# mLSTM and feed-forward on one core: a new order for the first group, a sigmoid moved, the second weights after the gates

## The chip, the cores and the metric

The kernel runs on one core of a Trainium2 chip. A core has five engines that run side by side, each on its own queue of instructions: TensorE (PE: matrix products, with PEld for its weight loads), VectorE (DVE), ScalarE (ACT), GpSimd (POOL) and SyncE (SP), which here only issues DMAs. The metric is the device time of one execution in microseconds. Before the change the median of three runs is 504.06 us (502.53 to 504.66).

## The reference, cut to what matters

Four batches with eight heads, 768 tokens and head dimension 40 go through an mLSTM recurrence; its output, 3072 tokens of 320 channels, goes through a feed-forward layer of width 2048. All is float32.

```python
def _attn_ref(q, k, v, i_gate, f_gate, o_gate):
    for t in range(S):
        m_new = np.maximum(f_gate[:, :, t] + m, i_gate[:, :, t])
        f_stab = np.exp(f_gate[:, :, t] + m - m_new)
        i_stab = np.exp(i_gate[:, :, t] - m_new)
        C = f_stab * C + i_stab * outer(v_t, k_t)
        n = f_stab * n + i_stab * k_t
        h_tilde = C @ q_t
        denom = np.maximum(np.abs(n . q_t), 1.0)
        o = 1.0 / (1.0 + np.exp(-o_gate[:, :, t]))
        y[:, :, t] = o * h_tilde / denom

def _moe_ref(x, w_in, w_out, alpha):
    h = x @ w_in
    g = np.maximum(h, 0.0) + alpha * np.minimum(h, 0.0)
    return g @ w_out
```

(The products with axes are abbreviated.)

## The kernel before, in words

**Attention.** Each batch is cut into 6 chunks of 128 tokens (n = 0 to 23 over all batches, c is the chunk within its batch, b the batch). Within a chunk the recurrence becomes a masked product: scores pS = K q, times a decay matrix E, times v; from the chunks before comes a state C. For each chunk stage_a makes q and k by channel (transposes on PE, copies on ACT), and stage_b makes, in two parities of four heads, the decay (exponentials L418 on ACT, a mask L422 on POOL), the scores on PE and their weighing, then the values pH (PE). gated_steps (L377) divides by the denominator, multiplies by the sigmoid of the output gate, og, (L392, on DVE, on POOL from chunk 6 on) and writes x as xn (L394), whose last 64 channels it copies once more behind themselves (L398, on POOL). From chunk 6 on the operands are split into three bfloat16 parts: score_parts (L322) and values_by_parts (L331), with casts on ACT (L327) in between.

**The output gate's sigmoid** is taken for a whole batch of six chunks at once by open_gate (L124): in stage_b, at the batch's first chunk, after the second parity's mask. Its data is loaded by load_gate when the batch before has ended, as there is one buffer. Exp and Sigmoid use different function tables of ACT; L126 is preceded by a table load, and so is the next Exp. Batch 0 takes it in two pieces in the opening order (og1, og2).

**Feed-forward.** Two chunks form a group g of 256 tokens (GC = 2, 12 groups). stage_x transposes x and splits it into high and low parts (XH, XL, X2, X2L). FeedForward.up (L576) makes in each of 8 steps fp two blocks of 128 hidden channels, eight products each (L585 to L592), then Relu on ACT (L594), the negative slope on DVE (L598), a high part gh on ACT (L606) and a low part gl (L607, on DVE for g < 2, on POOL after that). FeedForward.down (L610) adds into po (L615).

**Weights.** w_in comes in blocks of 512 columns (two row tiles wi and the remaining rows wr), w_out in pairs of 128 rows (wo). Each is fetched as raw words, and Weights.scale (L688, ACT), join in two steps (L700 and L702, DVE), high (L710, ACT) and low (L714, DVE) convert it. w[0], w[1], w[2] are block 0 of w_in (w[2] holds the remaining rows of blocks 0 and 1), w[3] and w[4] are block 1. The raw words lie in rooms shared with other weights, so the load of block 2's remaining rows waits until w[3]'s raw words have been read.

**The opening.** first_group (L803) builds the gates (cumulative sums L, decays) and the first group. Its steps have names, and the string ORDER (L559) says in which order they are issued. pin (L778) chains all of these instructions on each engine in that order, SP's DMAs included; queue (L790) puts everything issued until feed-forward step 2 behind the last of them. Beyond that the scheduler of the framework chooses the order on each engine. A step warmN (L939) issues N bfloat16 products of the identity into a PSUM tile that nobody reads. The steps that the text speaks of: dq, dv, dw, do, dx, dL are loads; lf, li, L, bj, wt are rows of the gates; qT/qc and kT/kc transpose and copy q and k; sp spreads a row of L over the partitions (PE, L890), ex takes its exponentials (ACT, L901), ms masks them (POOL, L905), sc are scores, wg weighs them (DVE, L925); bT, wT, eT turn gates to columns; wd is k weighed (kd, L139), u0 the state's update; v0 and v1 the values; g0r to g1p the steps of gated_steps; x0, x1 the transposes of x; s0, s1 their split (L481 to L485); w0 to w2 the conversions of weights; lpa to lpe split the sums of chunks 2 and 3. row and pick are copies of parts of the identity (L840, L841) that the spreads of chunks 1 to 3 use as weights.

After ORDER, first_group makes the rest of the gates for chunks 2 to 5 (L1099 to L1114); before the change the conversions of block 1 of w_in stand ahead of that (L1093 to L1095).

Of the kernel before, what the change touches and what calls it, by code (L numbers as in the profile page):

```python
# [8 lines left out]
F32 = mybir.dt.float32  # L9
# [8 lines left out]
def kernel(ctx: ExitStack, tc: tile.TileContext, q, k, v, i_gate, f_gate, o_gate, w_in, w_out, alpha, out):  # L18
# [105 lines left out]
    def open_gate(b, c0=0, c1=NC):  # L124
        og = o_tiles[b][:, c0:c1]
        nc.scalar.activation(og, og, AF.Sigmoid)  # L126
# [168 lines left out]
    def values(n, E, busy=lambda: None):  # L295

        pH = psa(f"pH{n}")
        va = va_t[n // GC % NV][:, n % GC]
        for i in range(H):
            if i % 2 == 0:  # L300
                busy()
            par, p = divmod(i, NPR)
            h = 2 * p + par
            nc.tensor.matmul(
                pH[:, h * VA : (h + 1) * VA], E[par][:, p * P : (p + 1) * P], va[:, h], start=True, stop=True
            )
        return pH[:, : H * VA].rearrange("p (h e) -> p h e", e=VA)
# [64 lines left out]
    def gated(n, hv):  # L372

        for _ in gated_steps(n, hv):
            pass

    def gated_steps(n, hv):  # L377
# [19 lines left out]
        yield  # L397
        nc.gpsimd.tensor_copy(xn[:, j, DM:], xn[:, j, 2 * P : DM])  # L398
        yield

    def stage_b(n):
# [4 lines left out]
        for par in range(2):  # L406
# [18 lines left out]
            )  # L425
            if c == 0 and par == 1:
                open_gate(b)
            pS = psa(f"pS{n}_{par}")
# [18 lines left out]
        if c > 0:  # L447
            *_, T = from_state(n, qf, Q)
        hv = values(n, Es) if n < NBF else values_by_parts(n, Es)
        if c > 0:  # L450
            nc.vector.tensor_tensor(T, T, hv, ALU.add)
            hv = T
        gated(n, hv)
        if c == NC - 1 and n + 1 < B * NC:
            load_gate(b + 1, nc.sync)
# [57 lines left out]
    def attention(n0):  # L513
# [44 lines left out]
    V0, V1 = 0, 2  # L558
    ORDER = """dq0 dq1 dw0 dw2 warm24 dv0 dw1 dw4 do1 dw3 do2 scan lf0a lf0b li0 lf0z L0 bj0 qT0 qc0 kT0 kc0 warm12 sp00  # L559
        bTt bTc l3a l3b alT l3c l3d warm6 wt0 ex00 sc00 l3e ms00 warm3 sp01 ewj ex01 ms01 sc01 warm3 eeL wg00 wTt eTt  # L560
        wTc eTc lf1a lf1b warm3 w0s wg01 sp10 alC ex10 ms10 warm3 sp11 ex11 qT1 w1s kT1 kc1 w0j0 warm4 li1 wd0 w0j1 w2s
        u0m qc1 u0c v0 w0h w0l w1j0 L1 w2j0 warm2 sc10 w1j1 warm2 w2j1 wd1 wg10 fsm fst sc11 ms11 warm6 dv1 dq3 wg11 og1
        lpa lpb bj1 dq2 dL dx2 w1h g0r dx0 g0g lpc lpd lpe g0x g0p w1l dx1 v1 x0 warm4 tadd g1r g1g s0a w2h g1x g1p w2l x1
        s1a s1d warm3 s0d og2"""

# [237 lines left out]
    def first_group():  # L803
# [34 lines left out]
        row = const.tile([3 * BH, BH], F32R, tag="row", name="row")  # L838
        for j in range(3):
            nc.vector.tensor_copy(row[j * BH : (j + 1) * BH], ident[j * BH : (j + 1) * BH, j * BH : (j + 1) * BH])  # L840
        nc.vector.tensor_copy(pick, row.bitcast(F32))  # L841

# [170 lines left out]
        def later_decays():  # L1013
# [16 lines left out]
        steps.update(  # L1030
            scan=scan_m,

            lf0z=lambda: nc.vector.memset(lf[0][:, 0:1], 0.0),
            lf0a=lambda: first_lf(0, t0, nc.vector), lf0b=lambda: second_lf(0, u0, nc.vector),
            lf1a=lambda: first_lf(1, t1, nc.gpsimd), lf1b=lambda: second_lf(1, u1, nc.gpsimd),
            li0=lambda: nc.gpsimd.tensor_tensor(li[:, t0], i[:, t0], m[:, u0], ALU.subtract),
            li1=lambda: nc.gpsimd.tensor_tensor(li[:, t1], i[:, t1], m[:, u1], ALU.subtract),
# [54 lines left out]
        weights(GC, NC, nc.gpsimd)  # L1092
        for t in w[3:]:  # L1093
            t.all()
        w[2].split(1)  # L1095
        yield


# [13 lines left out]
        nc.tensor.matmul(pg[:R, : BH * NC], ones, gd.rearrange("p a c -> p (a c)"), start=True, stop=True)  # L1112
        nc.vector.tensor_copy(gamB[:R].rearrange("p a c -> p (a c)"), pg[:R, : BH * NC])
        update(1)  # L1114
        yield
# [88 lines left out]
```

## Time and profile before

| | |
|---|---|
| median of three runs | 504.06 us |
| lowest and highest | 502.53 and 504.66 us |
| the profiled execution's own time | 500.96 us |
| its span, first to last instruction | 499.2 us |
| mean granted clock of TensorE in it | 0.99 |
| instructions | 11801 |

The profile is of one execution. The span is what the engines' rows add up in; 1.76 us of the execution lie around it. PE's granted clock is a share of 2.4 GHz: 1.00 is 2.4 GHz, 0.50 is 1.2 GHz. A row's idle time in brackets is what its engine waited just before it, with the name of what ended the wait, as far as semaphores tell it.

### The profile page before, as it was taken

Reading aid. Unit: us, or ns where it says so; the run is one execution under the profiler, and the core shown is the slowest. Engines: PE = TensorE matmul, PEld = TensorE weight load, DVE = VectorE, ACT = ScalarE, POOL = GpSimd, SP = SyncE. Lnnn points to the kernel's source line nnn. Section 1 sums busy time; section 2 is a strip of 40 time slices with the busy share of each in tenths; the row PEclk is TensorE's granted clock in tenths of the full one; section 3 lists DMA queues with packets and bytes.
Section 4 is the critical chain, followed back from the end, with each engine's and each line's share of the span. In section 5 each row is a group of like instructions: output and inputs, shape, how many; then the busy total and the mean of one; then the engine's idle time right before and its main releaser. Section 6 shows DMA issues by size and latency. Waiting matters only on the chain.

```text
span 499.2 us, 11801 instructions
## 1 busy us (share of the span) xinstructions
PE 477.7 (96%) x4463; PEld 457.2 (92%) x4463; DVE 321.6 (64%) x676; ACT 321.6 (64%) x700; POOL 304.8 (61%) x393
## 2 busy tenths in 40 slices
PE   8889889989999999999899999999999999999997
PEld 7778879989989999989799999989999999999997
DVE  6889999934577686764395686567586575642321
ACT  3869697656587677756976677677886673343332
POOL 6632262306469889839498789858878755243242
PEclk9989997999999999999999999999999999999999
DMA  9999976345676566597557575769663130000000
GB/s 169 228 189 278 229 203 183 82 79 125 145 181 146 92 166 156 102 166 158 116 143 135 129 141 121 162 166 156 117 175 83 32 97 1 1 27 1 28 1 26
DMA packets 173922, 61.60 MB, mean 123 GB/s; under 512 B 140154, under 2 KB 166122, under 8 KB 173866
## 3 DMA queue, kind: packets, MB, share of 16 engines
q1 hardware_dynamic: 173786, 60.75, 55.3%
q8 instruction: 35, 0.57, 0.5%
q14 instruction: 21, 0.17, 0.1%
q10 hardware_dynamic: 80, 0.11, 0.1%
HBM read 36.90 MB, written 4.03 MB: 82 GB/s over the span
## 4 chain that ended last, share of the span: by engine, by line
PE 62%; DVE 8%; DMA 8%; ACT 8%; SPq 6%; issue 3%; POOL 3%; ACTq 0%; DVEq 0%; POOLq 0%
PE po L615 25%; PE ph L585 4%; PE ph L588 3%; PE ph L586 3%; PE ph L589 3%; PE ph L591 3%; PE ph L587 3%; PE ph L592 3%; PE ph L590 3%; DMA wo<-in_moe_w_out_dram 3%; PE pH L340 3%; PE pS L434 2%; SPq L678 2%; ACT E L418 2%; SPq L122 2%
## 5 line engine op out<-in xcount | busy, mean ns | idle before, releaser
L607 POOL TENSOR_TENSOR gl<-g,gh 128x512 fp32r<-128x512 f32 x80 | 102.9, 1287 | 62.2 <-ACT gh L606 55.0
L598 DVE SCALAR_TENSOR_TENSOR g<-g,oma,ph 128x256 f32<-128x256 f32 x160 | 69.8, 476 | 76.9 <-ACT g L594 73.1
L615 PE MATMUL po<-OH,gh 128*128 128x320 f32 x368 | 111.3, 314 | 0.0
L615 PE MATMUL po<-OL,gh 128*128 128x320 f32 x368 | 109.6, 311 | 0.0
L594 ACT ACTIVATE g<-ph 128x512 f32<-128x512 f32 x96 | 57.2, 596 | 43.7 <-PE ph L592 31.8
L615 PE MATMUL po<-OH,gl 128*128 128x320 f32 x368 | 71.9, 316 | 1.3 <-POOL gl L607 1.3
L606 ACT CAST gh<-g 128x512 fp32r<-128x512 f32 x80 | 49.5, 619 | 33.3 <-DVE g L598 32.0
L615 PEld LDWEIGHTS po<-OH,gh 128*128 128x128 f32 x368 | 69.0, 188 | 0.4 <-ACT gh L606 0.2
L615 PEld LDWEIGHTS po<-OL,gh 128*128 128x128 f32 x368 | 69.2, 188 | 0.2 <-DVE OL L714 0.2
L585 PE MATMUL ph<-XH,WH 128*128 128x256 f32 x192 | 58.5, 305 | 1.3 <-DVE g L598 0.9
L615 PEld LDWEIGHTS po<-OH,gl 128*128 128x128 f32 x368 | 56.9, 188 | 1.8 <-POOL gl L607 1.8
L418 ACT ACTIVATE E<-Lb,bT 128x128 f32<-128x128 f32 x160 | 50.9, 393 | 7.5 <-PE pH L340 7.2
L589 PE MATMUL ph<-X,W 128*128 128x256 f32 x192 | 55.2, 288 | 0.0
L586 PE MATMUL ph<-XH,WH 128*128 128x256 f32 x192 | 54.9, 286 | 0.0
L588 PE MATMUL ph<-XH,WL 128*128 128x256 f32 x192 | 54.6, 284 | 0.0
L591 PE MATMUL ph<-XL,WH 128*128 128x256 f32 x192 | 54.6, 284 | 0.0
L592 PE MATMUL ph<-X2L,W 128*128 128x256 f32 x192 | 54.5, 285 | 0.0
L587 PE MATMUL ph<-XH,WL 128*128 128x256 f32 x192 | 54.4, 284 | 0.0
L590 PE MATMUL ph<-XL,WH 128*128 128x256 f32 x192 | 54.2, 282 | 0.0
L422 POOL TENSOR_SCALAR_AFFINE_SELECT E<-E 128x512 f32<-128x512 f32 x44 | 30.0, 683 | 36.4 <-ACT E L418 36.4
L327 ACT CAST E<-pS 128x512 bf16<-128x512 f32 x72 | 41.8, 585 | 13.9 <-DVE pS L325 9.1
L585 PEld LDWEIGHTS ph<-XH,WH 128*128 128x128 f32 x192 | 36.6, 191 | 2.3 <-issue 1.1
(198 smaller groups left out, 1146.0 us busy)
## 6 DMA issues: line engine op xcount, KB each, us to landing
Lb<-L_d SPq DMA_DIRECT2D x20, 512.0 KB
wo<-in_moe_w_out_dram SPq DMA_DIRECT2D x8, 640.0 KB
wi<-in_moe_w_in_dram SPq DMA_DIRECT2D x8, 512.0 KB
qn<-in_q_dram SPq DMA_DIRECT2D x24, 160.0 KB
kn<-in_k_dram SPq DMA_DIRECT2D x24, 160.0 KB
va<-in_v_dram SPq DMA_DIRECT2D x24, 160.0 KB
og<-in_o_gate_dram SPq DMA_DIRECT2D x24, 160.0 KB
out_dram<-ob SPq DMA_DIRECT2D x11, 320.0 KB
```

The costliest lines, as they stand in the source:

```text
L418: nc.scalar.activation(E[:, p * P : (p + 1) * P], Lb[:, h] if Lb is not None else pb[:, p * P : (p + 1) * P], AF.Exp, bias=bT[:, c, b * H ...
L585: nc.tensor.matmul(dst, WH[half][:, 0, hs], XH[:, 0], start=True, stop=False)
L586: nc.tensor.matmul(dst, WH[half][:, 1, hs], XH[:, 1], start=False, stop=False)
L587: nc.tensor.matmul(dst, WL[half][:, 0, hs], XH[:, 0], start=False, stop=False)
L588: nc.tensor.matmul(dst, WL[half][:, 1, hs], XH[:, 1], start=False, stop=False)
L589: nc.tensor.matmul(dst, W2[:, fs], X2, start=False, stop=False)
L590: nc.tensor.matmul(dst, WH[half][:, 0, hs], XL[:, 0], start=False, stop=False)
L591: nc.tensor.matmul(dst, WH[half][:, 1, hs], XL[:, 1], start=False, stop=False)
L592: nc.tensor.matmul(dst, W2[:, fs], X2L, start=False, stop=True)
L598: nc.vector.scalar_tensor_tensor(out=y[:, e], in0=gt[:, e], scalar=oma[:, f : f + 1], in1=ph[:, e], op0=ALU.mult, op1=ALU.add)
L607: (nc.vector if g < 2 else nc.gpsimd).tensor_tensor(gl, y, gh.bitcast(F32), ALU.subtract)
L615: nc.tensor.matmul(po[j], x[:, e, j * P : (j + 1) * P], W[f // NB][:, f % NB], **ends)
```

## The change: what it does

Six edits:

- gated_steps: the copy of x's last channels is done by DVE instead of POOL in group 0.
- stage_b: open_gate for a batch's first chunk moves from the second parity to behind the values, and is taken in two pieces: chunks 0 and 1 ahead of the gating, chunks 2 to 5 behind it.
- ORDER is another one. 24 warming products at its head become 12; both q are transposed ahead of the first spread; the later q, k, scores and masks of chunk 1 come before the values of chunk 0; ten warming products stand between the transposes of x's two halves.
- row and pick are copied by ACT, as a step rowc of ORDER, instead of by DVE ahead of it.
- li0 moves from POOL to DVE.
- The conversions of block 1 of w_in move behind the rest of the gates.

```diff
@@ gated_steps @@
-        nc.gpsimd.tensor_copy(xn[:, j, DM:], xn[:, j, 2 * P : DM])
+        (nc.vector if g == 0 else nc.gpsimd).tensor_copy(xn[:, j, DM:], xn[:, j, 2 * P : DM])
@@ stage_b @@
-            if c == 0 and par == 1:
-                open_gate(b)
             pS = psa(f"pS{n}_{par}")
...
         hv = values(n, Es) if n < NBF else values_by_parts(n, Es)
+
+        if c == 0:
+            open_gate(b, 0, GC)
         if c > 0:
             nc.vector.tensor_tensor(T, T, hv, ALU.add)
             hv = T
         gated(n, hv)
+        if c == 0:
+            open_gate(b, GC, NC)
@@ ORDER @@
-    ORDER = """dq0 dq1 dw0 dw2 warm24 dv0 dw1 dw4 do1 dw3 do2 scan lf0a lf0b li0 lf0z L0 bj0 qT0 qc0 kT0 kc0 warm12 sp00
-        bTt bTc l3a l3b alT l3c l3d warm6 wt0 ex00 sc00 l3e ms00 warm3 sp01 ewj ex01 ms01 sc01 warm3 eeL wg00 wTt eTt
-        wTc eTc lf1a lf1b warm3 w0s wg01 sp10 alC ex10 ms10 warm3 sp11 ex11 qT1 w1s kT1 kc1 w0j0 warm4 li1 wd0 w0j1 w2s
-        u0m qc1 u0c v0 w0h w0l w1j0 L1 w2j0 warm2 sc10 w1j1 warm2 w2j1 wd1 wg10 fsm fst sc11 ms11 warm6 dv1 dq3 wg11 og1
-        lpa lpb bj1 dq2 dL dx2 w1h g0r dx0 g0g lpc lpd lpe g0x g0p w1l dx1 v1 x0 warm4 tadd g1r g1g s0a w2h g1x g1p w2l x1
-        s1a s1d warm3 s0d og2"""
+    ORDER = """dq0 dq1 dw0 dw2 rowc warm12 dv0 dw1 dw4 do1 dw3 do2 scan lf0a lf0b lf0z L0 li0 bj0 qT0 qc0 kT0 kc0 warm3
+        qT1 qc1 warm10 l3a l3b sp00 bTt bTc sp01 wt0 ewj ex00 l3c l3d wTt l3e wTc ms00 sc00 ex01 wd0 wg00 ms01 kT1 lf1a w0s
+        sc01 warm2 u0m wg01 lf1b eeL sp10 u0c kc1 eTt w0j0 ex10 sp11 eTc w0j1 ms10 warm2 sc10 ex11 ms11 sc11 warm2 v0 wg10
+        L1 w1s fsm og1 wg11 alT w1j0 alC g0r li1 wd1 fst w0h w1j1 bj1 dv1 dq3 v1 lpa g0g g0x g0p lpb w2s w0l warm4 x0 tadd
+        g1r g1g g1x g1p s0a warm10 lpc lpd lpe w2j0 dq2 dL dx0 dx1 dx2 w1h x1 w2j1 s1a w2h s0d w1l s1d w2l warm6 og2"""
@@ first_group @@
-        for j in range(3):
-            nc.vector.tensor_copy(row[j * BH : (j + 1) * BH], ident[j * BH : (j + 1) * BH, j * BH : (j + 1) * BH])
-        nc.vector.tensor_copy(pick, row.bitcast(F32))
+
+        def picks():
+            for j in range(3):
+                nc.scalar.copy(row[j * BH : (j + 1) * BH], ident[j * BH : (j + 1) * BH, j * BH : (j + 1) * BH])
+            nc.scalar.copy(pick, row.bitcast(F32))
...
-            li0=lambda: nc.gpsimd.tensor_tensor(li[:, t0], i[:, t0], m[:, u0], ALU.subtract),
+            li0=lambda: nc.vector.tensor_tensor(li[:, t0], i[:, t0], m[:, u0], ALU.subtract),
...
         weights(GC, NC, nc.gpsimd)
-        for t in w[3:]:
-            t.all()
-        w[2].split(1)
-        yield
...
         nc.vector.tensor_copy(gamB[:R].rearrange("p a c -> p (a c)"), pg[:R, : BH * NC])
+        for t in w[3:]:
+            t.all()
+        w[2].split(1)
+        yield
         update(1)
```

## Rows read from the trace of the kernel before

**Rows 1.** The page's first part: busy us, share of the span, instructions, by engine.
```profile
PE 477.7 (96%) x4463; PEld 457.2 (92%) x4463; DVE 321.6 (64%) x676; ACT 321.6 (64%) x700; POOL 304.8 (61%) x393
```

**Rows 2.** Windows: length, busy us of PE, PEld, DVE, ACT, POOL; clock, DMA share, GB/s.
```profile
12.00:33.00 21.00, 17.33 (x157) 14.99 (x157) 18.32 (x36) 14.06 (x32) 12.37 (x14) 0.99 1.13 224
33.00:45.00 12.00, 11.18 (x104) 10.01 (x103) 9.89 (x25) 10.93 (x22) 1.40 (x2) 0.87 0.77 225
45.00:70.00 25.00, 23.17 (x213) 21.36 (x211) 23.54 (x47) 20.27 (x49) 9.04 (x11) 1.00 0.92 229
```

**Rows 3.** Windows again: two at the lower clock, three around later sigmoids.
```profile
32.60:36.00 3.40, 3.40 (x18) 3.40 (x17) 2.59 (x8) 3.36 (x5) 0.00 (x0) 0.50 0.33 120
...
73.60:80.40 6.80, 6.80 (x34) 6.80 (x34) 6.71 (x13) 6.67 (x16) 3.04 (x4) 0.50 0.99 294
...
106.00:111.00 5.00, 3.39 (x26) 3.13 (x25) 1.09 (x2) 4.06 (x4) 0.00 (x0) 1.00 0.00 2
...
236.00:243.00 7.00, 4.70 (x45) 4.40 (x44) 1.88 (x4) 5.10 (x8) 3.12 (x5) 1.00 0.69 128
...
346.00:354.00 8.00, 8.00 (x89) 7.75 (x86) 4.01 (x11) 7.86 (x17) 5.56 (x8) 1.00 1.14 200
```

**Rows 4.** PE's waits: line waited for, us in total, times, longest.
```profile
PE pH L340 <- ACT E L327: 3.6, 3, 2.3
...
PE po L615 <- ACT gg L606: 1.6, 1, 1.6
```

**Rows 5.** Timeline of ACT at sigmoids: start, us, instruction [idle before, releaser].
```profile
106.30 1.28 ACT L126 ACT_TABLE_LOAD   x1 [1.53 <-DMA og<-in_o_gate_dram]
107.59 1.80 ACT L126 ACTIVATE og<-og 128x1920 f32<-128x1920 f32 x1
...
237.94 1.28 ACT L126 ACT_TABLE_LOAD   x1 [1.89 <-DMA C<-C]
...
349.49 1.28 ACT L126 ACT_TABLE_LOAD   x1
```

**Rows 6.** Timeline of PE up to the first spread.
```profile
1.43 4.67 PE L942 MATMUL warm<-ident 128*128 128x256 bf16 x24 [1.43 <-POOL ident masks.py:199]
...
6.89 1.47 PE L942 MATMUL warm<-ident 128*128 128x256 bf16 x12
...
8.29 1.15 PE L890 MATMUL pb<-g_L,ident 32*128 32x128 f32 x8
```

**Rows 7.** Timeline of ACT: its first copy and first exponentials.
```profile
6.57 0.58 ACT L874 COPY qf<-pqk 104x512 f32<-104x512 f32 x1 [3.56 <-PE pqk L218]
...
9.83 1.14 ACT L901 ACTIVATE E<-pb,bT 128x128 f32<-128x128 f32 x4 [1.56 <-DVE bT L860]
```

**Rows 8.** Timeline of DVE from wT to the last split of x.
```profile
14.34 0.22 DVE L860 COPY wT<-ps_gw 128x64 f32<-128x64 f32 x1 [1.61 <-PE ps_gw L856]
...
15.96 3.02 DVE L139 TENSOR_TENSOR kd<-kn,wT 128x320 f32<-128x320 f32 x1
...
21.87 1.21 DVE L978 TENSOR_TENSOR_SCAN g_L<-g_WL,g_lf 32x512 f32<-32x512 f32 x1
...
29.99 0.49 DVE L394 TENSOR_TENSOR xn<-T,og 128x320 f32<-128x320 f32 x1
...
32.55 0.28 DVE L485 TENSOR_TENSOR X2L<-p,X 128x128 fp32r<-128x128 f32 x1
```

**Rows 9.** Timeline of POOL beside DVE's kd.
```profile
17.55 1.08 POOL L1037 TENSOR_TENSOR g_li<-g_WH,g_WL 32x512 f32<-32x512 f32 x1
```

**Rows 10.** Timeline of PE: first products of feed-forward steps 1 and 3.
```profile
32.29 0.39 PE L585 MATMUL ph<-XH,WH 128*128 128x256 f32 x1
...
43.02 0.39 PE L585 MATMUL ph<-XH,WH 128*128 128x256 f32 x1
```

**Rows 11.** Timeline of ACT: the sigmoid that ends the order.
```profile
31.87 1.27 ACT L126 ACTIVATE og<-og 128x1280 f32<-128x1280 f32 x1
```

**Rows 12.** Timeline of SP's queue: the load of block 2's remaining rows.
```profile
34.95 1.11 SPq L678 DMA_DIRECT2D wr<-in_moe_w_in_dram  x2
```

More of the change, by code (lines that the diff above doesn't have):

```diff
@@ L1030, in first_group @@
         steps.update(
-            scan=scan_m,
+            rowc=picks, scan=scan_m,
             lf0z=lambda: nc.vector.memset(lf[0][:, 0:1], 0.0),
```

## The prediction

> **What bounds the kernel now.** I read the busy shares first. TensorE is busy 96% of the 499.2 us span [rows 1], so only its idle time, and time at the lower clock, can be won. The windows by stage say where that lies. From 12 to 33 us, where the first group's x is made by an order written out by hand, DVE is busy 18.32 of 21.0 us and PE 17.33, much of it warming products. From 33 to 45 us ACT is busy 10.93 of 12.0; from 45 to 70 us DVE has 23.54 of 25.0 [rows 2]. So until some 95 us PE waits for DVE and ACT, which convert weights beside their own work, and after that PE is the bound. Two stretches ran at a granted clock of 0.50 (1.2 GHz): 32.6 to 36.0, after PE had mostly waited for x, and 73.6 to 80.4, in which 34 products took 6.8 us [rows 3]. In the late part two windows stand out: 106 to 111 (PE 3.39 of 5.0 us) and 236 to 243 (4.70 of 7.0) [rows 3]. The list of who waited names both: po for the cast gg on ACT, 1.6 us once, and pH for the cast E on ACT, 3.6 us in three waits, the longest 2.3 [rows 4]. ACT's own timeline shows why: at 106.30 and 237.94 it stands at the table load for a batch's sigmoid, after 1.53 and 1.89 us of idling for data, and then is occupied 1.28 + 1.80 us; the casts sit behind it in order. At 349.49 the same pair came without idling, and PE lost nothing there: from 346 to 354 it was busy 8.00 of 8.0 us [rows 3, 5].
>
> **The change, part by part.**
>
> *Before 12 us.* The four copies that make row and pick go from DVE to ACT. ACT idles 3.56 us before its first copy at 6.57 [rows 7]; even at the 0.58 us of that 104x512 copy the four take 2.3, so they cost nothing; if something uses up that cover, at most 2.3 us on the next item. li0 moves from POOL to DVE ahead of bj0: about 0.4 us of DVE while PE is not yet ready for bj0, so nothing. PE's order is what counts: 12 warming products open instead of 24, then two q transposes and one of k, 13 warming products, and only then spread(0,0). Now 12 products take 1.47 us and the spread 1.15 from 8.29 [rows 6]. With the second q transposed first (four products; the spread's eight took 1.15, so about 0.5) and its load issued behind k's, I get the spread from 8.9 to 10.05, the bias columns at 10.6 and the first exponential from about 10.7, against 9.83 [rows 7]: 0.9 us later. It is won back at once: the second exponential now follows directly, and wT is ready by 12.0 instead of 14.34 [rows 8].
>
> *12 to 33 us, DVE's list.* The same work goes through DVE, so I sum it as one list. Before it starts about 12 and ends with X2L at 32.55 + 0.28 = 32.83 [rows 8]. The window row gives 18.32 us in 36 instructions [rows 2]. Out of these: the copy of wT and most of bT, 0.47 us. In: two tail copies of x (128x64), until now on POOL; DVE's 128x64 copy took 0.22 [rows 8], so 0.4 us. One instruction was stretched: kd on DVE took 3.02 us at 15.96, while a 128x320 product of two SBUF operands took 0.49 at 29.99 [rows 8]; POOL ran one operation after another then, li1 at 17.55 the last before kd's end [rows 9]. In the new order kd stands at about 12.0, beside a single mask of POOL, so I take off 2.5. That leaves 18.32 - 0.47 + 0.4 - 2.5 = 15.75 us. But other instructions with two SBUF operands now meet POOL: the scan L1 (1.21 us at 21.87 with POOL idle [rows 8]) comes at some 18.4, when POOL's queue holds mask, li1 and kd of chunk 1 back to back. What that costs the trace does not show for this place. From below it is 0 (or up to 0.5 better, since the 18.32 holds small stretches too); from above the 2.5 us that kd paid, the nearest row. I take 1.0. Idle between the instructions was 21.0 - 18.32 = 2.7 us, 1.61 of it one wait for wT [rows 2, 8]; that wait goes, but two new ones come, for scores(0,1) and for the mask of chunk 1, which I work out at 0.7 each from PE's and ACT's orders: 2.3 in all. Sum: 12.0 + 15.75 + 1.0 + 2.3 = 31.05, against 32.83: 1.8 us earlier. With the two ends for L1 and 0.8 us either way for the waits the gain lies between -0.5 and 3.6.
>
> Here the skill speaks against the change. The Trainium skill (SBUF — State Buffer, "Who interferes with whom") says that a VectorE instruction with two SBUF inputs and a GpSimd instruction that reads SBUF exclude each other, and the later one blocks wholly. The trace agrees as far as kd's 3.02 us shows [rows 8, 9]. By it the scan could lose all of li1 and kd, some 2 us, and the gain of this stage would be 0.8.
>
> *x and the first products.* The tail copies of x, which PE's last transposes wait for, no longer change engines; on DVE they cost 0.2 us each, counted above. The ten warming products between x's transposes take about 1.2 us, in which PE has nothing else: DVE must still do the five steps of the second chunk's gating, about 2.1 us. Were x earlier than that they would hold PE by what is left of them. With them PE should stay at 2.4 GHz where it had 0.50 from 32.6 to 36.0 [rows 3], which is 1.7 us of PE's time. The first product can start near 29 instead of 32.29 [rows 10], but the low parts it needs end with DVE's list at 31. So PE is up to 3.5 us ahead after the second block of columns, and DVE and ACT are 1.8 to 2 ahead: the sigmoid that ends this order on ACT (31.87, 1.27 [rows 11]) should come about 2 us earlier. As these two set the pace until 95 us, I count their shift: 1.9 us. PE's surplus turns into waits.
>
> *The rest of the gates first.* The second block's conversions now stand behind a table load, three exponentials and their copies. The cast and scale work of that block is the same; it comes some 2.7 us of ACT later than it could. PE came to its first use, the third feed-forward step, at 43.02 [rows 10], after the attention's products; with ACT's part of these conversions about 3 us (five passes of some 0.6) behind the gates' 2.7 from 31, and DVE's lagging by one, I get it ready near 39 to 40, so nothing. If those products no longer lie between, PE waits about 1 us. On SP v, q, k and L keep their places. The load wr of the third block waited until 34.95 for a conversion of this block [rows 12]. It will wait for it again, and v, L and the next weights queue behind it; the two loads of output weights, now ahead of it, come earlier. Both are used much later than they land, so nothing; if not, about the 1 us by which wr moves.
>
> *The sigmoid.* In batches 1 to 3 it goes behind the values, a half chunk later, cut into 128x640 (ahead of the gating) and 128x1280 (behind). The table loads stay as many. Its data should then have landed, so ACT no longer idles 1.53 and 1.89 us, and casts wait for 2.0 and then 1.3 us instead of 4.6 and 5.0 [rows 5]. PE's gaps there were 1.6 and 2.3 [rows 4], together 3.9. A block of 3.1 us at 349.49 cost nothing [rows 3], so I expect most of them gone and take 3.0. The ends are a gain of 3.9 and the loss that the third rival works out, as the gating now waits for the sigmoid, on POOL.
>
> Sum: 1.9 + 3.0 = 4.9 us off the profiled execution: 500.96 us (the span 499.2 and 1.76 around it) becomes 496.1. The median of the three runs, 504.06, lies 3.1 above that execution; taken off the median it is **499.2 us**.
>
> **The rivals.**
> *The early gain is eaten* in the DVE-bound stretch: DVE's 23.54 of 25.0 us [rows 2] leaves no room, a collision with POOL takes 1 to 2 us, and of the sigmoid's only half is kept. For it: kd's row; against it: the list gets shorter by kd's stretch. 504.06 - 0.4 - 1.6 = 502.
>
> *A cold start.* 24 warming products took 4.67 us, 0.195 each, and the next twelve 0.122 [rows 6]: PE began at the lower of its clocks. With twelve it stops near 4 us and waits for q. If the clock is not up then, three transposes (1.5 by the above), 13 products (1.5), the spread and the bias (1.4) run at 1.2 GHz: up to 4.4 us more, ahead of everything. The early gain turns into a loss of 2.5; with the sigmoid's 3.0 that is 503.5. For it: half the opening work; against it: even the twelve keep PE busy for some 2.5 us at that level, and the next products follow within 2 us. The Trainium skill (TensorE: Matmul & The Clock Gate, "What's actually happening") says the same way round that the clock starts throttled and activity releases it; the two per-product times above agree.
>
> *Slower: the gating holds POOL.* For chunks 6, 12 and 18 POOL's product og x r waits for the sigmoid, and the low parts gl (POOL's from the third group on) queue behind it; PE's po waits for those. Price: 1.28 + 0.74 for load and first half, and two casts of 0.58 ahead of them on ACT, 3.2 us a time. It decides once PE loses more than (1.9 / 3) 0.6 us a time. With two thirds of the price, 6.4, and no gain from the sigmoid: 504.06 - 1.9 + 6.4 = 508.6. Against it: the low part is used two steps after it is made, and r needs some time itself.
>
> *Better:* the stretch at 1.2 GHz from 73.6 to 80.4 [rows 3] followed a wait of PE for DVE; with DVE ahead it may not come. It is worth about 3 us, since nearly all of its 34 products ran at half the clock: 496.
>
> **How the numbers follow.** Forecast 0.45, better 0.17, early gain eaten 0.18, cold start 0.10, POOL held 0.10. What a measurement of this kernel can tell from no change is about 0.5%, 2.5 us. Faster by more: the better case, nine tenths of the forecast, a third of the eaten one: 0.64. Slower by more: most of the POOL case, 0.09. The rest, 0.27, is within. The forecast's own range is 496.5 to 501.5; the range from 494.5 to 505.0 takes in the better case, the eaten gain and the cold start, and leaves out the POOL case.
>
> **What would show it.** The last X2L on DVE near 31 us, kd on DVE under 1 us, the first L585 near 29 and no granted clock of 0.50 before 36; a first exponential (L901) near 10.7, not 12; no PE gap over 1 us at the sigmoids of batches 1 and 2, and og products on POOL without long idling before them. Wrong if PE's idle time after 95 us is as large as before, or if the scan L1 takes over 3 us.

## The result, and the profile after

The changed kernel takes **505.24 us** (median of 20 runs, 502.72 to 508.32) beside 502.12 (20 runs, 500.24 to 505.36) for the kernel before on the same chip: a ratio of 1.006, 95% interval 1.004 to 1.008. It is slower by some 3 us; 499.2 was forecast, in a range that ended at 505.0. The forecast stood on 504.06, the median of three runs before, 1.9 us above that of 20; what was forecast is a gain of 4.9, what came is a loss of 3.1. The profiled execution has a span of 503.4 us against 499.2.

The busy shares after, engine by engine, answer to [rows 1]: they hardly differ, so the page alone does not say where the time went.

```profile
PE 478.7 (95%) x4439; PEld 458.2 (91%) x4439; DVE 319.9 (64%) x675; ACT 325.6 (65%) x709; POOL 302.5 (60%) x390
```

The windows that answer to [rows 2] and [rows 3] (length, busy us of PE, PEld, DVE, ACT, POOL, granted clock, DMA share, GB/s), with one more, from 320 to 385 us, which matters below:

```profile
12.00:33.00 21.00, 17.92 (x163) 16.20 (x162) 19.28 (x40) 13.91 (x35) 11.89 (x12) 0.97 1.13 230
33.00:45.00 12.00, 10.51 (x88) 8.95 (x86) 9.41 (x22) 10.10 (x18) 2.79 (x2) 0.78 0.93 215
45.00:70.00 25.00, 24.06 (x204) 23.62 (x205) 22.13 (x44) 18.22 (x45) 7.26 (x10) 0.86 0.77 199
...
106.00:111.00 5.00, 5.00 (x40) 4.90 (x40) 2.27 (x4) 3.78 (x6) 0.00 (x0) 1.00 0.27 45
236.00:243.00 7.00, 6.61 (x64) 6.32 (x63) 3.84 (x8) 6.73 (x13) 5.07 (x6) 1.00 0.76 133
...
320.00:385.00 65.00, 61.20 (x623) 58.63 (x622) 41.17 (x87) 48.81 (x103) 46.75 (x59) 1.00 0.60 129
```

Read three things. PE's gaps in the two windows at the first two sigmoids are gone: busy 5.00 of 5.0 and 6.61 of 7.0 us, against 3.39 and 4.70 [rows 3]. The opening has not got shorter: DVE is busy 19.28 us, against 18.32 [rows 2], and PE's clock from 33 to 70 us is lower than before. And 320 to 385 us has lost what the sigmoids gave: PE is busy 61.20 us there, where the kernel before has 64.12:

```profile
320.00:385.00 65.00, 64.12 (x658) 61.89 (x657) 44.54 (x96) 49.06 (x109) 50.91 (x66) 1.00 0.66 142
```

Why the opening is not shorter is on DVE's timeline after (start, us, instruction, and idle time before it with what ended it), to be held against [rows 8]. Line numbers move a little between kernels: L465 and L587 here are L462 and L585 of the kernel before.

```profile
13.50 0.23 DVE L864 COPY wT<-ps_gw 128x64 f32<-128x64 f32 x1
13.76 0.92 DVE L139 TENSOR_TENSOR kd<-kn,wT 128x320 f32<-128x320 f32 x1
...
19.94 2.08 DVE L982 TENSOR_TENSOR_SCAN g_L<-g_WL,g_lf 32x512 f32<-32x512 f32 x1
...
28.26 0.72 DVE L392 TENSOR_TENSOR og<-og,r 128x320 f32<-128x320 f32 x1
29.02 1.22 DVE L394 TENSOR_TENSOR xn<-T,og 128x320 f32<-128x320 f32 x1
30.27 0.20 DVE L398 COPY xn<-xn 128x64 f32<-128x64 f32 x1
...
32.90 0.28 DVE L488 TENSOR_TENSOR X2L<-p,X 128x128 fp32r<-128x128 f32 x1
```

The list starts late: wT is copied at 13.50, not at 12.0 as forecast. kd has shrunk from 3.02 to 0.92 us, as worked out. But the scan has grown from 1.21 to 2.08, and xn, which took 0.49 before, takes 1.22. What ran beside both is on POOL's timeline:

```profile
19.86 1.08 POOL L1041 TENSOR_TENSOR g_li<-g_WH,g_WL 32x512 f32<-32x512 f32 x1
20.91 1.63 POOL L139 TENSOR_TENSOR kd<-kn,wT 128x320 f32<-128x320 f32 x1
...
27.97 0.66 POOL L1030 TENSOR_TENSOR LP<-L_later 32x256 bf16<-32x256 f32 x1 [3.39 <-ACT L_later L1026]
28.71 1.17 POOL L852 TENSOR_TENSOR g_WL<-g_WH,g_L 32x512 f32<-32x512 f32 x1
```

The scan overlaps two POOL instructions, of 1.08 and 1.63 us; og overlaps one of 0.66 and xn one of 1.17. PE's timeline shows who pays: the transposes of the second half of x (x1) wait 2.07 us for xn, after ten warming products that took 1.25, and the products behind them run at half speed, 0.41 us where a like one takes 0.28.

```profile
27.05 1.25 PE L946 MATMUL warm<-ident 128*128 128x256 bf16 x10
30.38 0.53 PE L465 MATMUL p<-ident,xn 128*128 128x128 f32 x3 [2.07 <-DVE xn L394]
...
32.42 0.41 PE L588 MATMUL ph<-XH,WH 128*128 128x256 f32 x1
```

The windows around it give the clock: 1.00 up to 30.4 us with PE almost idle at the end, then two stretches near 0.50 (1.2 GHz), 13.7 us in all, against 3.4 in this part before [rows 3]. (These are two single executions; over all timed runs it is otherwise, as shown below.)

```profile
28.30:30.40 2.10, 0.03 (x2) 0.05 (x1) 2.03 (x4) 0.64 (x2) 1.50 (x2) 1.00 1.44 154
31.50:38.40 6.90, 6.90 (x34) 6.48 (x34) 4.81 (x12) 6.77 (x11) 0.00 (x0) 0.51 0.76 297
45.20:52.10 6.90, 6.16 (x30) 6.09 (x31) 6.74 (x12) 5.65 (x14) 2.27 (x3) 0.51 1.18 273
```

### The profile page after: what moved, and what is told of

It reads as the page before. It is cut to its first block, busy times and chain, and to the rows that moved or that the text cites. A ratio compares the mean times of both kernels' runs of the same rounds, so it can differ in the third digit from the quotient of the medians.

```text
span 503.4 us, 11753 instructions
## 1 busy us (share of the span) xinstructions
PE 478.7 (95%) x4439; PEld 458.2 (91%) x4439; DVE 319.9 (64%) x675; ACT 325.6 (65%) x709; POOL 302.5 (60%) x390
## 4 chain that ended last, share of the span: by engine, by line
PE 57%; DVE 11%; ACT 10%; DMA 9%; POOL 7%; issue 5%; SPq 1%; ACTq 0%; DVEq 0%; POOLq 0%
PE po L617 22%; PE ph L587 4%; PE ph L590 3%; PE ph L588 3%; PE ph L591 3%; PE ph L589 3%; PE ph L593 3%; PE ph L594 3%; PE ph L592 3%; DMA kS<-Z 3%; DMA qS<-Z 2%; ACT E L418 2%; PE pH L340 2%; PE pS L432 2%; POOL gl L609 2%
## 5 line engine op out<-in xcount | busy, mean ns | idle before, releaser
L587 PE MATMUL ph<-XH,WH 128*128 128x256 f32 x192 | 59.0, 307 | 6.1 <-DVE g L600 4.3
L587 PEld LDWEIGHTS ph<-XH,WH 128*128 128x128 f32 x192 | 36.9, 192 | 7.7 <-issue 3.6
```

Source lines behind the costliest of these rows:

```text
L587: nc.tensor.matmul(dst, WH[half][:, 0, hs], XH[:, 0], start=True, stop=False)
```

## The experiments

Each kernel was timed beside the kernel before on the same chip; times are medians of 12 runs, ratios are to the kernel before, with 95% intervals. An executed kernel varies by several us from run to run (the kernel before from 497.1 to 507.3, with medians of 501.0 to 501.9 on the five occasions), so verdicts go by the ratios; profiles, one execution each, say how.

Behind the opening the framework's scheduler chooses the order on each engine anew for every kernel, and a small edit can change it far from its place. Going by the instructions of DVE, ACT, POOL, SP and PE in their order of start, e9 and e15 differ from the changed kernel in nothing but the warming products, e14 likewise from the kernel before, e13 from e5 and e16 from e11. Others are not so clean: e4 has another order than the changed kernel from 56 to 108 us, e12 than e18 from 55 to 106, e8 than e3 from 56 to 101, e6 and e10 than e3 from 35 to 110, e17 than e6 from 34 to 104, e5 than the kernel before from 28 to 98. What these show of their one edit is shown together with the new order there.

### Which part of the change costs

**e1_sigmoid**: the kernel before plus the moved sigmoid.

```
 stage b, after affine_select:  - if c == 0 and par == 1: open_gate(b)
 before / after gated(n, hv):   + open_gate(b, 0, GC) / open_gate(b, GC, NC), at c == 0
```

> The kernel before with the sigmoid's move alone. Theory A (the sigmoid's move is worth something, the opening eats it): PE's gaps of 1.6 us at 108 and 2.3 us at 240 go, 2 to 3.5 us faster than before, some 499. Theory B (cut in two, the sigmoid lets exponentials in between and pays more table loads): a gain at the first two and a loss of 2 to 4 us in the last batch, so within 1.5 us of before, and at least two table loads more on ACT.

**e2_gates**: the kernel before plus the rest of the gates ahead of the second block of weights (the loop over w[3:] goes from behind weights(GC, ...) to ahead of update(1)).

> The kernel before with only the rest of the gates put ahead of the second block of weights. If that is what costs: PE waits over 1 us between 38 and 46, a granted clock of 0.50 follows near 45, and the time is 2 to 3 us above before. If it is free, as the prediction had it: within 1 us of before.

**e3_order**: the changed kernel with these two put back; what is left is the new order with its three changes of engine.

> The changed kernel with the sigmoid and the second weights put back where they were: the new order, its copies on ACT and DVE. If the new order's cold start (0.50 from 7.7 us) is the loss: bias columns copied near 12.2 us, first feed-forward product near 32, 2 to 3 us above before. If the order is neutral and the other two edits cost: within 1 us of before.

**e4_warm24**: the changed kernel with the 24 opening warming products of before.

```
-dw2 rowc warm12 dv0
+dw2 rowc warm24 dv0
```

> The changed kernel with 24 instead of 12 warming products at its head. If the cold start costs: no granted clock of 0.50 before 12 us, bias columns copied near 10.6 instead of 12.2, DVE's list of the first group 1.5 us earlier, and 1.5 to 2.5 us faster than the changed kernel, some 503. If what happens before 12 us is taken back by waits for DVE and ACT later: within 0.7 us of the changed kernel.

Measured: e1 502.33 (1.0014, 0.9979 to 1.005); e2 502.66 (0.9999, 0.9958 to 1.0039); e3 506.66 (1.0082, 1.0049 to 1.0115); e4 505.16 (1.0068, 1.0032 to 1.0105). The new order makes the whole loss: the sigmoid and the gates, moved alone, make none, and with both put back the loss stays. e4 by itself does not clear the cold start, since its order differs as well. But e18 below does: its profile shows the start as cold (first exponential at 12.20 us, against 12.42 in the changed kernel and 10.79 in e4), and it is the fastest kernel of all.

### What in the order costs

**e5_engines**: the old order with the new engines. **e6_order_pool**: the new order with li0 and the tails of xn back on POOL.

```
-(nc.vector if g == 0 else nc.gpsimd).tensor_copy(xn[:, j, DM:], ...)
+nc.gpsimd.tensor_copy(xn[:, j, DM:], ...)
-li0=lambda: nc.vector.tensor_tensor(li[:, t0], ...)
+li0=lambda: nc.gpsimd.tensor_tensor(li[:, t0], ...)
```

> The kernel before with its own order, and only the changes of engine that the new order brought along: li of the first block and the two copies of xn's tail go from POOL to DVE, the four copies of the pick matrix from DVE to ACT. Theory A, DVE's load: DVE is busy for 14.8 of 15 us between 70 and 85 us and is the engine that ends last in the opening; li (about 1 us) and two tails (about 0.5 us each) more on it come straight out of the path, so this kernel takes 1.5 to 4 us more than the kernel before (503.5 to 506 beside 502). Theory B, the sequence: it is the order of the steps that costs, and this kernel stays within 1.5 us of the kernel before. Theory C, the clock after the gap at x1: as B, since here the two halves of x stand where they stood.

> The new order alone (sigmoid and second weights where they were before), with li of the first block and the tail copies of xn back on POOL; the pick copies stay on ACT. The new order alone had taken 506.66 beside 501.88. Theory A, DVE's load: 2 to 4 us of this come back, 502.5 to 504.5. Theory B, the sequence: 505.5 to 507.5; a tail on POOL, behind the exponentials' mask there, may even make x1 later than the 2.07 us gap. Theory C, the clock after x1's gap: as B.

**e8_warm**: e3 with 24 warming products at the start and 24 between the halves of x.

```
-dw2 rowc warm12 dv0 ... s0a warm10 lpc
+dw2 rowc warm24 dv0 ... s0a warm24 lpc
```

> The new order alone, with 24 warming products at the start instead of 12 and 24 instead of 10 between the two halves of x, which cover the 2.07 us wait of x1 for xn. Theory C, the clock: TensorE's granted clock falls to 0.50 for 6.8 us right after that wait in each of three executions (from 29.06, 30.54 and 31.56 us), while the first products of the feed-forward run; covered, 2 to 4 us come back, 502.5 to 504.7 beside 506.7 for the new order alone. Theories A and B: DVE is late whatever TensorE's clock is, the time stays at 505.5 to 507.5.

Measured: e5 499.14 (0.994, 0.9906 to 0.9974); e6 501.63 (1.0008, 0.9975 to 1.0041); e8 500.93 (0.998, 0.9954 to 1.0006). Theory A as I had put it fell: with the copies on DVE the old order is not slower but faster. Yet in the new order putting two of them back takes 4 us away by the ratios, and more warming, which moves no data at all, takes 5. The two meet in one place, the wait ahead of x1. All three lie below every range named for them. The next two change one thing each in the program. (Of the three low stretches named in e8's expectation, e3's was 3.4 us long, not 6.8.)

**e9_x1warm**: the changed kernel, `s0a warm10 lpc` to `s0a warm24 lpc`. **e10_tail**: e3 with only the tail copies back on POOL.

> The changed kernel with one number different: 24 warming products instead of 10 between the two halves of x; the opening keeps its 12. With 24 in both places the new order alone had gone from 506.7 to 500.9, with 24 at the start alone (in the changed kernel) from 505.2 only to 505.2. Theory C, the clock behind x1's wait for xn: this kernel takes 500.5 to 502.5, and its granted clock stays at 1.00 from 25 to 36 us. Rival, both colds must be mended together, or what helped was a shift of everything later by chance: 504 to 506.

> The new order alone with only xn's tail copies back on POOL; li of the first block stays on DVE. With both back it took 501.6 beside 506.7. Theory D: a tail on POOL stands in front of POOL's gating of the second block (li less L, 1.2 us), which thereby starts only when xn is written, and so no longer stretches DVE's product for og (0.49 to 0.72 us) and xn (0.49 to 1.22 us) in front of x1; x1's wait falls from 2.07 us to about 0.6 and the clock holds: 501 to 503. Rival: it was li on DVE, 1 us on the path to the first exponential: the time stays at 505 to 507.

Measured: e9 **499.49** (0.9965, 0.9936 to 0.9994), e10 501.41 (0.9999, 0.9972 to 1.0026); e9 is 1 us below its range, e10 within. One number is worth some 5 us (ratios 1.006 and 0.9965), and here nothing else differs, the order of all other instructions included. e6 and e10 differ in li0 alone, and in time not at all: of the two moves it is the tail copies that matter. DVE and POOL of e10, the same instructions as above: the second tail copy now stands in POOL's queue and waits 1.39 us for xn, and the rest of the gating (here L1028, L850) stands behind it. So og and xn take 0.49 us again.

```profile
26.49 0.49 DVE L392 TENSOR_TENSOR og<-og,r 128x320 f32<-128x320 f32 x1
27.02 0.49 DVE L394 TENSOR_TENSOR xn<-T,og 128x320 f32<-128x320 f32 x1
```

```profile
27.57 0.37 POOL L398 COPY xn<-xn 128x64 f32<-128x64 f32 x1 [1.39 <-DVE xn L394]
28.02 1.09 POOL L1028 TENSOR_TENSOR LP<-L_later 32x256 bf16<-32x256 f32 x1
29.18 1.45 POOL L850 TENSOR_TENSOR g_WL<-g_WH,g_L 32x512 f32<-32x512 f32 x1
```

The Trainium skill (SBUF — State Buffer, "Who interferes with whom") says that VectorE with two SBUF inputs and GpSimd hold one port by turns; xn's 1.22 us beside POOL and 0.49 without agree. In e9 xn comes as late behind the first half of x as before (x1 starts 3.3 us after the warming products do in both), but PE runs 24 products meanwhile, and what is left of the wait is 0.54 us:

```profile
26.20 2.78 PE L946 MATMUL warm<-ident 128*128 128x256 bf16 x24
29.52 0.53 PE L465 MATMUL p<-ident,xn 128*128 128x128 f32 x3 [0.54 <-DVE xn L394]
...
31.23 0.28 PE L588 MATMUL ph<-XH,WH 128*128 128x256 f32 x1
```

The window from 28.5 to 34.5 us, in the changed kernel and then in e9, shows the clock at 0.75 and 1.00, and 23 products against 38 (x1 also starts 0.86 us earlier in e9, whose opening was less late in this execution):

```profile
28.50:34.50 6.00, 4.12 (x23) 3.66 (x24) 5.56 (x12) 3.93 (x6) 1.30 (x2) 0.75 1.15 315
```

```profile
28.50:34.50 6.00, 4.71 (x38) 3.82 (x36) 4.74 (x11) 4.31 (x7) 0.52 (x1) 1.00 1.12 341
```

It is 1.00 in e6, e8 and e10 too, and 0.72 and 0.55 in e3 and e4.

### Is it the clock, or any shift of the program?

**e15_behind**: the changed kernel with 14 more warming products directly behind x1 (`x1 w2j1` to `x1 warm14 w2j1`), the ten ahead of it as they were. **e17_cold**: e6 without the ten warming products ahead of x1 (`s0a warm10 lpc` to `s0a lpc`); no data waits for them, but the scheduler's order is another from 34 us on.

> The changed kernel with its 10 warming products ahead of x1 as they were and 14 more directly behind x1's transposes, in front of the first products of the feed-forward. Theory C, the wait ahead of x1 lowers the clock: the wait stays 2.07 us, the clock falls near 31 us as before, the 14 products themselves run partly at half speed, and nothing comes back: 504.5 to 507. Rival, any 14 products there shift the program into a better arrangement: 500 to 502.5.

> The new order alone with li and xn's tails back on POOL (501.6, no loss), and the ten warming products between the two halves of x left out; nothing waits for them, so every other instruction can start as it did. TensorE then idles some 1.9 us ahead of x1 instead of 0.62. If idling there is what costs (by the granted clock of the first feed-forward products): 504.5 to 507, with a granted clock of 0.50 from about 30 us. If it is the arrangement of the other engines' work: 500.5 to 503.

Measured: e15 500.91 (0.9977, 0.9943 to 1.0011). My expectation missed, and the rival's number came out. The wait is still 2.07 us and the clock falls at 30.71, but it is back at 34.13, after 3.4 us instead of 6.8, and the second stretch does not come at all. That the 14 products cut it short is not shown: in e3, which has none of them, the clock was back after 3.4 us too. So covering the wait is not the only mend. e17: 503.37 (1.0036, 1.0000 to 1.0072), against 1.0008 for e6, with overlapping intervals. By the ratios e17 is 1.4 us slower than e6, by medians against the kernel before, on both occasions, 2.5 (503.37 - 501.04 against 501.63 - 501.77), in neither of its two ranges and not clear of noise. Its clock is as expected:

```profile
28.10:34.90 6.80, 5.63 (x26) 4.79 (x27) 6.44 (x13) 6.04 (x11) 2.48 (x3) 0.50 1.14 336
41.80:48.50 6.70, 6.12 (x41) 5.68 (x42) 6.34 (x13) 4.01 (x10) 1.59 (x3) 0.50 1.03 228
```

All twelve of its runs had a mean clock of 0.972 to 0.983; e6's had 0.980 to 0.997. So without the ten products the clock is lower, run after run. What that costs stays open, as the order differs too.

How far is the clock the reason, then? The mean granted clock of all timed runs gives an estimate. Half of a stretch at 0.50 is lost if nothing hides it, so what the mean lacks of 1.00, times the span, is the time that the low clock takes at most: 7.8 us in the changed kernel (mean 0.985), 5.7 in e9 (0.989), 5.8 in e15 (0.989). That is 2 us between kernels that lie 4 to 5 apart. In the kernel before the mean was 0.981 to 0.984 on the five occasions, not higher than in the changed kernel, though the two profiled executions had 0.990 and 0.979. And e17, with the lowest mean of all (0.978), is by its ratio (1.0036) not slower than the changed kernel (1.006) or e3 (0.984, 1.0082). So the clock explains part of what e9 gains, some 2 us if each kernel loses time in step with it, and not why the changed kernel is slower than the kernel before.

### The sigmoid

**e7_sig12**: the kernel before with the sigmoid moved in batches 1 and 2 only (`b != B - 1` at the new places, `b == B - 1` at the old).

> The kernel before, with the sigmoid moved ahead of the gating in batches 1 and 2 alone; batch 3 opens its gate where it did. Theory: the moved sigmoid takes away waits of 1.6 us at 108 us and 2.3 us at 240 us and gives about 3 us back in batch 3, where an exponential table stands between its halves and TensorE runs behind ACT. Then this kernel takes 2 to 4 us less than the kernel before, 498 to 500 beside 502. Rival: the waits at the first two gates are those for the gate's load, which starts only when the batch before has left its buffer; they move and don't go, and the time stays within 1 us of 502.

Measured: 499.99 (0.996, 0.9929 to 0.9991), within the forecast; but only one of its two waits is gone. In the window from 106 to 111 us the longest is now 0.61 us instead of 1.61. The one near 242 us stands as it did, before and in e7:

```profile
242.69 0.23 PE L340 MATMUL pH<-vb,E 128*128 128x126 bf16 x1 [2.30 <-ACT E L327]
```

```profile
242.28 0.21 PE L340 MATMUL pH<-vb,E 128*128 128x126 bf16 x1 [2.28 <-ACT E L327]
```

It is 2.28 us in e1 too, 2.03 in e9 and 0.39 in the changed kernel: in two kernels with the same order on every engine it can come or not. That much of the rival, that these waits move and don't go, came out. ACT idles 2.80 us for og's load there in e7, 1.50 in the changed kernel. With all three batches moved the gain is given back (e1, 1.0014). Lines of 320 to 385 us, e1 and then e7, against 64.12 before:

```profile
320.00:385.00 65.00, 62.84 (x628) 60.26 (x628) 41.04 (x88) 50.28 (x105) 48.69 (x64) 1.00 0.64 138
```

```profile
320.00:385.00 65.00, 64.08 (x657) 61.84 (x656) 44.54 (x96) 49.11 (x109) 50.59 (x64) 1.00 0.65 140
```

ACT's timeline of the changed kernel says why: in batch 3 the exponentials come between the two halves of the sigmoid, so the tables are loaded four times where the kernel before loaded two (2.6 us more of ACT), and the second half (354.19) comes where casts are wanted.

```profile
345.93 1.28 ACT L126 ACT_TABLE_LOAD   x1 [0.25 <-DMA og<-in_o_gate_dram]
347.23 0.74 ACT L126 ACTIVATE og<-og 128x640 f32<-128x640 f32 x1
...
348.76 1.28 ACT L418 ACT_TABLE_LOAD   x1
350.06 2.45 ACT L418 ACTIVATE E<-Lb,bT 128x128 f32<-128x128 f32 x8
...
352.89 1.28 ACT L126 ACT_TABLE_LOAD   x1
354.19 1.27 ACT L126 ACTIVATE og<-og 128x1280 f32<-128x1280 f32 x1
...
366.22 1.28 ACT L418 ACT_TABLE_LOAD   x1 [0.46 <-PE pH L340]
```

### Towards a faster kernel

**e11_best_old**: e5 plus e7. **e12_mended**: the changed kernel with 24 warming products in both places and batch 3's sigmoid at its old place. **e18_x1_sig12**: the same with 12 at the start.

> The kernel before in its own order with what has won by itself so far: the engines of li, the tails and the pick copies as in the new order (ratio 0.994) and the sigmoid moved in batches 1 and 2 alone (0.996). If the two add: 0.990, 497 beside 502. If both draw on the same slack (the wait for the gate's load at 108 us follows the opening, whose gain it then eats): 499 to 500.

> The changed kernel with three mends: 24 warming products at the start and between the halves of x, and the sigmoid of batch 3 where it was before. If the new order's loss is the clock behind x1 (about 5 us) and the sigmoid's is its split in batch 3 (2 to 3 us), this takes 498 to 500, less than the kernel before; if the loss lies in the sequence of conversions, which is unchanged here, 502 to 505.

> The changed kernel with 24 warming products between the halves of x (499.5 by that alone) and the sigmoid of batch 3 where it was before. If the split of batch 3's sigmoid costs here what it cost in the old order (0.4%, 2 us): 497 to 499. If its place makes no difference under this order and the 24 warming products at the start were what cost e12: 499 to 500.5. If the return of batch 3's sigmoid is what cost e12: 501.5 to 503.

Measured: e11 498.69 (0.995, 0.9921 to 0.9979), e12 502.22 (1.0003, 0.9977 to 1.0029), e18 **498.14** (0.9938, 0.9904 to 0.9973). e18, the changed kernel with two mends, is some 6 us below the changed kernel by the ratios and beats both. From 320 to 385 us its PE is busy 64.16 us. The gains do not add in e11. e12 missed its first forecast: with 24 products at the start it takes 0.65% more than e18, some 3 us. But the two differ in the scheduler's order from 55 to 106 us as well, and which of the two costs the time is not separated.

The old order has such a wait of its own: 1.74 us ahead of the first state products. **e14_before_warm** covers it (`w0j0 warm4 li1` to `w0j0 warm20 li1`), **e13_engines_warm** is the same on e5, **e16_old_all** on e11.

> The kernel before with that one number alone (20 warming products instead of 4 ahead of the first state products). Theory C: 498 to 500.5 beside 501.8, since many of its executions fall to 0.50 there. Rival, hidden or chance: 501 to 503.

> The old order with the new engines for li, the tails and the pick copies (499.14 by itself), and 20 warming products instead of 4 ahead of the first state products, where TensorE waits 1.75 us for kd and, in four of six profiled executions of the old order, its granted clock then falls to 0.50 for 10.24 us. Theory C, the clock behind a wait of the opening: half of a 10 us stretch at half speed is at most 5 us, of which the waits of the opening hide some; 495.5 to 498, with 1.00 from 18 to 31 us. Rival, what the opening loses there is hidden behind DVE and ACT, or the gains are chance: 498.5 to 501.

> The old order with the new engines, the sigmoid moved in batches 1 and 2 alone (498.69 together) and 20 warming products ahead of the first state products. If the gains add: 495 to 497. If the wait for the gate's load at 96 to 108 us takes them back: 498 to 500.

Measured: e14 500.36 (0.9979, 0.9946 to 1.0011), e13 500.03 (0.9959, 0.9929 to 0.9989), e16 498.86 (0.9938, 0.9907 to 0.9968). The clock holds at 1.00 up to 32 us or later in all three. In e13 and e16 the rival's numbers came out: against e5 (0.994) and e11 (0.995) they gain nothing that can be told from noise. e14's median lies in theory C's range, but its interval takes in 1. These three change nothing but the warming products, so they are clean: a covered wait was worth 5 us in the new order, and here 1 us or nothing. That the work behind this wait is hidden beside DVE's list is argued, not shown. The rows still teach something. First the kernel before, then e2, same order up to here: the wait and what follows it.

```profile
19.08 0.51 PE L161 MATMUL pu<-va,kd 128*40 128x42 f32 x16 [1.74 <-ACT kf L270]
...
20.90:30.90 10.00, 8.38 (x73) 7.31 (x72) 9.58 (x21) 5.00 (x9) 4.34 (x5) 1.00 1.26 170
```

```profile
19.83 0.51 PE L161 MATMUL pu<-va,kd 128*40 128x42 f32 x16 [1.75 <-ACT kf L270]
...
20.90:30.90 10.00, 10.00 (x49) 9.31 (x49) 6.52 (x14) 4.59 (x8) 3.87 (x4) 0.50 1.14 180
```

The same wait was followed by 10 us at 1.00 in one execution and at 0.50 in the other.

## Why the prediction was wrong

**The step that failed** first is the 1.9 us of the opening, at two places of its working; the second is the 3.0 us of the sigmoid. By the table below, the opening and what follows it up to the 128th product lost 2.6 us instead of gaining 1.9.

*"The tail copies of x ... no longer change engines; on DVE they cost 0.2 us each."* They did: 0.20. What the sum left out is who stood behind them on POOL. As long as a copy waits in POOL's queue for xn, POOL's gating of the later chunks waits too. With the copy gone it runs into og and xn, which grow by 0.23 and 0.73 us in front of x1. I had allowed 1.0 us for such a meeting at the scan (it cost 0.87) and none here. DVE's list ended at 33.18 (32.90 + 0.28), not 31.05, and the first L587 came at 32.04, not 29. Of these 2.1 us 1.5 had gone before the list began (wT at 13.50, not 12.0, behind the cold start; in e4, which has none, at 11.87); the list itself took 0.6 longer than summed. In e6 and e10, with the copies back, x1's wait was 0.61 us.

*"The ten warming products between x's transposes take about 1.2 us ... With them PE should stay at 2.4 GHz."* They took 1.25, but the gap was 1.25 + 2.07: the five gating steps that I put at 2.1 us took 2.96, until xn was done at 30.24. Even by the forecast's own figures, 1.2 us of products against 2.1 of gating, some 0.9 us of the gap stood uncovered; that PE stays at 2.4 GHz over it had no row behind it. After it the clock was at 0.50 for 6.8 us, and the forecast's +1.7 us for PE became a loss. e9 changed the number of products alone and got some 5 us back.

**The sigmoid's 3.0 us** was too much even at its two places. PE's busy time rose by 1.61 and 1.91 us in the windows at 108 and 240, but other waits came: all of PE's waits from 100 to 320 us fell by 2.1 (7.1 to 5.0), with a new one of 1.53 at 182 us among them. *"The table loads stay as many"* was wrong: batch 3 has two more, and 320 to 385 us lost 2.9. *"Its data should then have landed"* was wrong as well: ACT idled 0.81 and 0.69 us for og's load ahead of batch 1's two halves and 1.50 ahead of batch 2's. I had looked at the third block of [rows 5] only to see that it cost nothing where it stood, not at what it would meet where it went. So a sign of being wrong that the prediction named came true: PE's waits after 100 us are as large as before, 8.8 us against 8.0.

**Right:** kd under 1 us (0.92); wr and the weights' order free (e2, 0.9999); no harm from POOL held at the gate. **The cold start** came nearly as its rival described, 0.50 from 7.67 to 11.08 us and the first exponential at 12.42 instead of 9.83 [rows 7]:

```profile
12.42 1.92 ACT L905 ACTIVATE E<-pb,bT 128x128 f32<-128x128 f32 x7 [2.83 <-DVE bT L864]
```

Of the eight profiled executions with 12 products at the start, six have the first exponential between 11.60 and 12.42 us and two near 10.8. e15 and e18 began as late as the changed kernel (12.24 and 12.20) and were 4 and 6 us faster, so it does not make the loss; what it costs is not shown.

**Where the loss is in the end**, by the end of the n-th product into ph (feed-forward), against the kernel before, in us, one execution each:

```
                 after    e3    e6    e9   e15   e17   e18
128th product    +2.6   +3.3  -4.1  +0.4  +2.1  +2.4  +1.3
896th            +0.3   +3.7  -3.5  -2.1  -2.4  +3.4  -2.1
1088th           +4.0   +6.2  -0.1   0.0  -0.3  +3.9  -2.1
```

The changed kernel is 2.6 us late at the 128th product (99 us), level after two sigmoids, and loses 3.7 in batch 3, of which 2.1 is the move's (e9, e15; none in e18). The other 1.6 are two waits of ACT for the DMA that reads Z into qS, which are longer than in e9; the casts behind them are late, and PE waits 1.66 and 1.54 us instead of 0.91 and 0.66. First the changed kernel, then e9, with the same order on every engine:

```profile
331.89 0.46 ACT L230 CAST Z<-qn 128x320 bf16<-128x320 f32 x1 [2.11 <-DMA qS<-Z]
...
370.97 0.46 ACT L230 CAST Z<-qn 128x320 bf16<-128x320 f32 x1 [1.81 <-DMA qS<-Z]
```

```profile
328.77 0.46 ACT L230 CAST Z<-qn 128x320 bf16<-128x320 f32 x1 [1.35 <-DMA qS<-Z]
...
366.95 0.46 ACT L230 CAST Z<-qn 128x320 bf16<-128x320 f32 x1 [0.92 <-DMA qS<-Z]
```

e3 and e6, with the sigmoid at its old place, lose 2.5 and 3.4 there behind the same wait (2.42 and 2.65 us, against 1.33 in the kernel before). e6 shows what the new order can give: 4.1 us ahead at the 128th product, and nearly all of it gone after batch 3. Open stay why that DMA ends later in some kernels, and why e15, nearly as late as the changed kernel at the 128th product, is ahead by the 896th.

**What to carry to other kernels.** When an instruction leaves an in-order engine, look at what it held back there: the copy cost 0.2 us on DVE, and what it set free on POOL cost more, in front of the one wait that PE could not cover. Size warming products by the whole wait, and check the gap they leave in the trace. Before one edit is held responsible for a time, compare the order of the other instructions: a scheduler may have moved them. And take the mean clock from all runs, not from one profile. A table function that is moved must be followed at every batch, since another function between its halves costs two more loads (1.28 us each here).

## What was unexpected of the hardware

A wait of TensorE of 1.7 to 2.1 us could be followed by 3.4, 6.8 or 10.2 us at 0.50, or by none: after the 2.07 us wait the clock fell in all four profiled executions that had it (the changed kernel, e3, e4, e15), after the 1.74 us wait in five of the six profiled executions of the old order that had it uncovered, and not in the one read for the forecast. Even the same opening gave different lengths: 6.8 us in the changed kernel and e4, 3.4 in e3 and e15. And a DVE product of 128x320 took 1.22 us instead of 0.49 beside a POOL operation on only 32 partitions.
